# Casting loads on GpSimd's queue, pooling by TensorE, and a second matmul in weight-piece order, in a pooled-attention and feed-forward kernel

## The chip, the cores and the metric

The kernel runs on one core of a Trainium2 chip. The metric is the device time of one execution in microseconds (us), the median of several runs. A core has TensorE (PE, the matmuls; PEld is its loading of weights), VectorE (DVE), ScalarE (ACT), GpSimd (POOL) and SyncE (SP, which here only issues DMAs). A DMA is issued from the queue of one of these engines and carried out by 16 DMA engines that all queues share.

## The reference, cut to what matters

```python
# q, k, v: (8, 8, 576, 64) float32;  w_in: (512, 2048), w_out: (2048, 512) float32
k_p = k.reshape(B, H, Sp, 8, D).mean(axis=3)        # Sp = 72
v_p = v.reshape(B, H, Sp, 8, D).mean(axis=3)
scores = np.matmul(q, k_p.transpose(0, 1, 3, 2)) / np.sqrt(D)
attn = softmax(scores)                               # over the 72 pooled keys
x = np.matmul(attn, v_p)    # then heads side by side: (4608, 512)
h = x @ w_in                # (4608, 2048)
g = h * np.cos(h)
out = g @ w_out             # (4608, 512)
```

## The kernel before

Attention goes batch by batch (8 batches of 576 tokens), the two large matmuls go by tiles of 512 tokens (9 tiles, index t). Batch 0 is attended alone; then tile t runs `up` (first matmul, cosine, product: 8 groups `fp` of two 128-wide chunks, 64 matmuls) and the second matmul, "down" (64 matmuls `down_mm`, by token quarter `ms`, then by chunk `fc`), and between the matmuls of down stand the attention steps of batch t+1, by a hand-written list `fill` of positions (L281, L282). The order on each engine is the program's order; the framework adds the waits.

**Loads.** All loads are issued by SP, float32, into staging tiles: `kv_st` (three buffers, L49), `q_main` and `q_rem` (one each, L50), `w_st` (two, L48), in the order k0, q0, v0, four pieces of w_in, four of w_out, k1, q1, v1, k2 and so on. A weight piece is cast to bfloat16 by DVE (w_in, L259) or POOL (w_out, L264); with two buffers, the third piece is loaded only when the first is cast. q is cast by POOL (`cast_q`, L119, L121). k and v are pooled (8 rows summed) by three additions (L111 to L113): on DVE for batch 0, on POOL for the others.

**Attention of a batch.** `k_transpose` (L161) and `q_transpose` (L140: 16 transposes of 128x128, two heads each) and `q_transpose_rem` (L151) bring k and q to the layout that the matmuls want. Then eight steps: `scores` (L171) and an exponential on ACT (L174, `ex`); `values`, which multiplies `ex` by ones (L183: the sums) and by pooled v (L185), takes ACT's logarithm (L187, `lnc`) and exponential (L189, `inv`) of the sums, and multiplies on DVE (L191) into `xT`, the first matmul's input. `values` uses the one pair of PSUM banks, bank 2, so the next step's sums wait for this step's DVE product.

**Second matmul.** Down of a tile uses two PSUM banks in turn (`obanks`); a token quarter passes over all 16 chunks of `w_out_sb` before the next, so the first quarter already needs the whole of w_out.

Of the kernel before, what the change touches and what calls it, by code (L numbers as in the profile page):

```python
# [19 lines left out]
def kernel(  # L20
# [20 lines left out]
    NSTEP = 2 * KCH  # L41
    assert d_model == 512 and S == 576 and n_tokens % TILE == 0
# [12 lines left out]
    identity = consts.tile([128, 128], BF16, name="identity")  # L55
    make_identity(nc, identity)
    ones = consts.tile([128, D], BF16, name="ones")
    nc.gpsimd.memset(ones, float(POOL))
    half_pi = consts.tile([128, 1], FP32, name="half_pi")
    nc.gpsimd.memset(half_pi, math.pi / 2.0)  # L60

    w_in_sb = wpool.tile([128, KCH, d_ff], BF16, name="w_in_sb")
    w_out_sb = wpool.tile([128, FFCH, d_model], BF16, name="w_out_sb")
# [41 lines left out]
    def pool_kv(b, which, eng, halves=1):  # L105
        st = staged.pop((which, b))
        dst = asb.tile([Sp, H, D], BF16, name=f"{which}p", tag=f"{which}p")
        hs = H // halves
        for i in range(halves):
            s = st[:, i * hs:(i + 1) * hs]  # L110
            eng.tensor_tensor(out=s[:, :, 0:4, :], in0=s[:, :, 0:4, :], in1=s[:, :, 4:8, :], op=ADD)  # L111
            eng.tensor_tensor(out=s[:, :, 0:2, :], in0=s[:, :, 0:2, :], in1=s[:, :, 2:4, :], op=ADD)  # L112
            eng.tensor_tensor(out=dst[:, i * hs:(i + 1) * hs, :], in0=s[:, :, 0, :], in1=s[:, :, 1, :], op=ADD)  # L113
# [221 lines left out]
```

## Time and profile before

| | |
|---|---|
| median of 3 runs | 388.56 us (388.04 to 391.95) |
| profiled execution, own time | 387.81 us |
| its span, first to last instruction | 385.9 us |
| PE busy | 326.0 us (84%) |
| ACT, DVE, POOL busy | 191.9, 167.9, 141.3 us |
| DMA, mean over the span | 120 GB/s, 46.41 MB |
| chain that ended last | PE 75%, DMA 12%, DVE 4%, ACT 3%, POOL 3% |

The profile is one execution. The views used are the busy time by stage (windows of time), the chain of work that ended last in order of time, the timeline of instructions, and the DMA traffic of a stretch. Tile names are the program's, and L140 is line 140 of the kernel above.

### The profile page before, as it was taken

To read this page: it belongs to the slowest core of one execution; us is meant where nothing else is said; L and a number is where in the kernel's file an instruction comes from. 1 tells how busy PE (TensorE), PEld (TensorE's weight loads), DVE (VectorE), ACT (ScalarE), POOL (GpSimd) and SP (SyncE) were. 2 spreads that over 40 slices of the span, in tenths; PEclk is the share of its full clock that TensorE was granted. 3 is DMA by queue.
4 is the path that set the end of the run, shared out by engine and by line. 5 is a ranking of instruction groups with operands and counts; after the bars stand their busy time and mean duration, and the time that the engine had idled before them with its cause. 6 is when DMAs were issued, how large, how long until landed. Compare 5 with 4: busy or idle time off the path is not lost.

```text
span 385.9 us, 4455 instructions
## 1 busy us (share of the span) xinstructions
PE 326.0 (84%) x1728; PEld 134.5 (35%) x1728; DVE 167.9 (44%) x212; ACT 191.9 (50%) x280; POOL 141.3 (37%) x70
## 2 busy tenths in 40 slices
PE   0343775087999999999999999999999999999995
PEld 0211222042345234433443343245334433444442
DVE  2452365021357335622753374347335733642741
ACT  1056415014655766575657565656575576621620
POOL 0200033799927930990198049605850000000000
PEclk9999969568999999999999999999999999999999
DMA  7940689898368319821971395149420010002002
GB/s 187 238 159 0 219 288 282 189 191 196 107 157 191 93 38 204 183 63 59 219 175 27 104 217 132 54 124 197 102 56 27 2 54 27 29 27 75 8 27 82
DMA packets 31469, 46.41 MB, mean 120 GB/s; under 512 B 5337, under 2 KB 13529, under 8 KB 31449
## 3 DMA queue, kind: packets, MB, share of 16 engines
q1 hardware_dynamic: 31448, 46.14, 46.8%
q8 instruction: 13, 0.21, 0.3%
q14 instruction: 8, 0.06, 0.1%
HBM read 36.70 MB, written 9.44 MB: 120 GB/s over the span
## 4 chain that ended last, share of the span: by engine, by line
PE 75%; DMA 12%; DVE 4%; ACT 3%; POOL 3%; SPq 1%; issue 1%; POOLq 0%
PE obank L226 34%; PE bank L218 29%; DMA kv_st<-in_v_dram 5%; PE bank L183 4%; PE bank L171 3%; DMA q_main<-in_q_dram 3%; PE bank L185 2%; DMA w_st<-in_moe_w_in_dram 2%; PE bank L140 2%; DVE xT L191 2%; ACT inv L189 2%; ACT lnc L187 2%; DMA w_st<-in_moe_w_out_dram 1%; POOL kv_st L111 1%; DVE w_in_sb L259 1%
## 5 line engine op out<-in xcount | busy, mean ns | idle before, releaser
L226 PE MATMUL obank<-w_out_sb,g_sb 128*128 128x512 bf16 x576 | 151.5, 387 | 0.0
L218 PE MATMUL bank<-xT,w_in_sb 128*128 128x512 bf16 x576 | 130.6, 389 | 6.7 <-DVE g_sb L223 4.1
L222 ACT ACTIVATE cos<-bank,half_pi 128x1024 f32<-128x1024 f32 x72 | 80.3, 1115 | 78.4 <-PE bank L218 78.4
L223 DVE TENSOR_TENSOR g_sb<-bank,cos 128x1024 bf16<-128x1024 f32 x72 | 88.0, 1224 | 51.4 <-ACT cos L222 51.4
L111 POOL TENSOR_TENSOR kv_st<-kv_st 72x2048 f32<-72x2048 f32 x14 | 63.2, 4518 | 87.4 <-DMA kv_st<-in_k_dram 82.7
L218 PEld LDWEIGHTS <-w_in_sb 128*128 128x128 bf16 x576 | 57.4, 100 | 78.6 <-issue 10.6
L191 DVE TENSOR_TENSOR xT<-bank,inv 128x288 bf16<-128x288 f32 x64 | 29.3, 458 | 94.9 <-ACT inv L189 94.9
L174 ACT ACTIVATE ex<-bank 72x576 bf16<-72x576 f32 x64 | 40.8, 640 | 54.4 <-PE bank L171 53.4
L226 PEld LDWEIGHTS <-g_sb 128*128 128x128 bf16 x576 | 46.3, 98 | 58.3 <-issue 14.4
L187 ACT ACTIVATE lnc<-bank 128x288 f32<-128x288 f32 x64 | 26.3, 411 | 41.5 <-PE bank L185 41.5
L231 DVE COPY o_sb<-obank 128x512 f32<-128x512 f32 x36 | 24.8, 688 | 31.0 <-PE obank L226 31.0
L183 PE MATMUL bank<-ex,ones 72*64 72x288 bf16 x128 | 21.3, 324 | 15.7 <-DVE xT L191 15.2
L112 POOL TENSOR_TENSOR kv_st<-kv_st 72x1024 f32<-72x1024 f32 x14 | 32.9, 2349 | 1.1
L189 ACT ACTIVATE inv<-lnc 128x288 f32<-128x288 f32 x64 | 28.3, 442 | 2.0
L161 PE MATMUL bank<-identity,kp 72*128 72x72 bf16 x32 | 2.8, 208 | 26.0 <-POOL kp L113 14.7
L183 PEld LDWEIGHTS <-ones 72*64 72x64 bf16 x128 | 9.1, 109 | 41.4 <-issue 41.4
L185 PE MATMUL bank<-ex,vp 72*64 72x288 bf16 x128 | 20.6, 309 | 3.2 <-POOL vp L113 2.3
L264 POOL CAST w_out_sb<-w_st 128x2048 bf16<-128x2048 f32 x4 | 7.6, 1894 | 41.8 <-DMA w_st<-in_moe_w_out_dram 41.8
L171 PE MATMUL bank<-qT,kpT 64*72 64x288 bf16 x128 | 21.1, 329 | 1.0 <-DVE qT L143 1.0
L119 POOL CAST q_bf<-q_main 128x2048 bf16<-128x2048 f32 x8 | 15.1, 1889 | 11.8 <-DMA q_main<-in_q_dram 11.8
L171 PEld LDWEIGHTS <-kpT 64*72 64x72 bf16 x128 | 7.4, 110 | 27.7 <-issue 27.7
L143 DVE COPY qT<-bank 128x2048 bf16<-128x2048 bf16 x8 | 9.8, 1225 | 8.9 <-PE bank L140 8.9
(26 smaller groups left out, 96.4 us busy)
## 6 DMA issues: line engine op xcount, KB each, us to landing
q_main<-in_q_dram SPq DMA_DIRECT2D x8, 1024.0 KB
out_dram<-o_sb SPq DMA_DIRECT2D x32, 256.0 KB
kv_st<-in_k_dram SPq DMA_DIRECT2D x7, 1152.0 KB
kv_st<-in_v_dram SPq DMA_DIRECT2D x7, 1152.0 KB
w_st<-in_moe_w_in_dram SPq DMA_DIRECT2D x4, 1024.0 KB
w_st<-in_moe_w_out_dram SPq DMA_DIRECT2D x4, 1024.0 KB
kv_st<-in_k_dram SPq DMA_DIRECT2D x2, 576.0 KB
kv_st<-in_v_dram SPq DMA_DIRECT2D x2, 576.0 KB
```

The lines of the kernel that those rows point to most:

```text
L111: eng.tensor_tensor(out=s[:, :, 0:4, :], in0=s[:, :, 0:4, :], in1=s[:, :, 4:8, :], op=ADD)
L112: eng.tensor_tensor(out=s[:, :, 0:2, :], in0=s[:, :, 0:2, :], in1=s[:, :, 2:4, :], op=ADD)
L171: nc.tensor.matmul(pair[:Sp, hp, :SEG], lhsT=kpT[hp * 64:hp * 64 + 64, pj, :], rhs=qT[hp * 64:hp * 64 + 64, pj, sg * SEG:(sg + 1) * SEG])
L174: nc.scalar.activation(out=ex, in_=pair[:Sp, :, :SEG], func=ACTF.Exp, scale=scale / POOL)
L183: nc.tensor.matmul(cs[hp * 64:hp * 64 + 64, :], lhsT=ones[:Sp, :], rhs=ex[:, hp, :])
L187: nc.scalar.activation(out=lnc, in_=cs, func=ACTF.Ln)
L189: nc.scalar.activation(out=inv, in_=lnc, func=ACTF.Exp, scale=-1.0)
L191: nc.vector.tensor_mul(out=xT[:, pj, c0:c0 + SEG], in0=ao, in1=inv)
L218: nc.tensor.matmul(h[:, j, :], lhsT=w_in_sb[:, ki, fc * 128:(fc + 1) * 128], rhs=xT[:, ki, t * TILE:(t + 1) * TILE], start=(ki == 0), stop ...
L222: nc.scalar.activation(out=cos, in_=h, func=ACTF.Sin, bias=half_pi[:, :1])
L223: nc.vector.tensor_mul(out=g_sb[:, 2 * fp:2 * fp + 2, :], in0=h, in1=cos)
L226: nc.tensor.matmul(obanks[ms % 2], lhsT=g_sb[:, fc, ms * 128:(ms + 1) * 128], rhs=w_out_sb[:, fc, :], start=(fc == 0), stop=(fc == FFCH - 1))
```

## The change

- The weights, q of all batches, and k and v of batches 0 and 1 are loaded by DMAs issued from POOL's queue into bfloat16 tiles; the cast happens in the DMA. Casts on DVE and POOL and the staging of weights go. Each weight piece has a tile of its own (`w_in_sb[0..3]`, `w_out_sb[0..3]`), q has two buffers, the bfloat16 k/v four.
- k and v of batches 2 to 7 still come float32 from SP and are pooled by POOL. All k/v loads are split into partitions 0 to 63 and 64 to 71. The loads of k2 and v2 are now SP's first instructions, without a wait.
- k and v of batches 0 and 1 are pooled by TensorE: `pool_k_mm` (64 matmuls against the identity, 8 of them accumulating into one result, which comes out transposed) and `pool_v_mm` (8 matmuls of 512 columns).
- `q_transpose` now takes one head at a time: 32 transposes of 128x64 a batch in place of 16 of 128x128.
- Batch 0's attention uses all PSUM banks: scores run two steps ahead, the sums alternate between two banks, and the products with v follow four steps later.
- In tile 0, down goes by weight piece (`cg`), then token quarter, into four PSUM banks at once; batch 1's transposes and the pooling of v stand ahead of it, the pooling of k inside `up` behind fp 5.

```diff
-    wst = ctx.enter_context(tc.tile_pool(name="wst", bufs=2))
-    kvst = ctx.enter_context(tc.tile_pool(name="kvst", bufs=3))
-    qst = ctx.enter_context(tc.tile_pool(name="qst", bufs=1))
+    kvb = ctx.enter_context(tc.tile_pool(name="kvb", bufs=4))
+    kvst = ctx.enter_context(tc.tile_pool(name="kvst", bufs=2))
+    qst = ctx.enter_context(tc.tile_pool(name="qst", bufs=2))
     asb = ctx.enter_context(tc.tile_pool(name="asb", bufs=2))
     msb = ctx.enter_context(tc.tile_pool(name="msb", bufs=3))
...
+    def load_kv_cast(b, which, src, halves=1):
+        st = kvb.tile([Sp, H, POOL, D], BF16, name=f"{which}_b", tag="kv_b")
         hs = H // halves
...
+        for j in range(halves):
+            for o, i in by_rows(st[:, j * hs:(j + 1) * hs].rearrange("p h t d -> p h (t d)"),
+                                kv_view(src, b)[j * hs:(j + 1) * hs]):
+                nc.gpsimd.dma_start(out=o, in_=i.rearrange("h p n -> p h n"))
...
     def load_w_in(cg):
-        st = wst.tile([128, KCH, 512], FP32, name="w_st", tag="w_st")
-        nc.sync.dma_start(
-            out=st, in_=moe_w_in[:, cg * 512:(cg + 1) * 512].rearrange("(k p) f -> p k f", p=128))
-        return st
+        nc.gpsimd.dma_start(
+            out=w_in_sb[cg],
+            in_=moe_w_in[:, cg * 512:(cg + 1) * 512].rearrange("(k p) f -> p k f", p=128))
...
+    def pool_k_mm(b, bank, pjs):
+
+        kb = staged["k", b]
+        if ("kpT", b) not in att:
+            att["kpT", b] = asb.tile([128, KCH, Sp], BF16, name="kpT", tag="kpT")
+        ps = bank[:, 0:KCH * Sp].rearrange("p (j n) -> p j n", j=KCH)
+        for pj in pjs:
+            for t in range(POOL):
+                for hp in range(2):
+                    nc.tensor.matmul(ps[hp * 64:hp * 64 + 64, pj, :], lhsT=kb[:, 2 * pj + hp, t, :],
+                                     rhs=identity[:Sp, :Sp], start=(t == 0), stop=(t == POOL - 1))
+        sl = slice(pjs[0], pjs[-1] + 1)
+        nc.vector.tensor_copy(out=att["kpT", b][:, sl, :], in_=ps[:, sl, :])
+
+    def pool_v_mm(b, bank):
+        vb = staged["v", b]
+        for t in range(POOL):
+            nc.tensor.matmul(bank[:Sp, :], lhsT=identity[:Sp, :Sp], rhs=vb[:, :, t, :],
+                             start=(t == 0), stop=(t == POOL - 1))
+        dst = asb.tile([Sp, H, D], BF16, name="vp", tag="vp")
+        nc.vector.tensor_copy(out=dst, in_=bank[:Sp, :].rearrange("p (h d) -> p h d", h=H))
+        pooled["v", b] = dst
...
-        for t in range(4):
-            for pj in range(KCH):
-                nc.tensor.matmul(ps[:, t, pj, :], qb[:, t, 2 * pj:2 * pj + 2, :].rearrange("p h d -> p (h d)"),
-                                 identity, is_transpose=True)
+        for i, pj in enumerate(pjs):
+            for t in range(4):
+                for hp in range(2):
+                    nc.tensor.matmul(ps[hp * 64:hp * 64 + 64, i, t, :], qb[:, 2 * pj + hp, t, :],
+                                     identity, is_transpose=True)
...
+    load_kv_cast(0, "k", k, 2)
...
+    load_q(0, 2)
+    load_kv_cast(0, "v", v)
+    for cg in range(4):
+        load_w_in(cg)
+    load_kv_cast(1, "k", k)
+    load_q(1)
+    load_kv_cast(1, "v", v)
+    for cg in range(4):
+        load_w_out(cg)
+    load_kv(2, "k", k)
+    load_kv(2, "v", v)
...
+    LAG = 4
...
+    for i in range(NSTEP + LAG):
+        if i < NSTEP:
+            sums(0, i, obanks[i % 2])
+            inverse(0, i, obanks[i % 2])
+            if i + 2 < NSTEP:
+                scores(0, i + 2, banks[i % 2])
+        if i == LAG - 1:
+            pool_v_mm(0, banks[2][:, 0, :])
+        if i >= LAG:
+            values(0, i - LAG, banks[2][:, 0, :])
+            normal(0, i - LAG, banks[2][:, 0, :])
...
+            if t == 0 and fp == 5:
+                pool_k_mm(1, obanks[0], range(KCH))
...
+        if t == 0:
+            outs = [obanks[0], obanks[1], banks[2][:, 0, :], banks[2][:, 1, :]]
+            mms = [(ms, fc) for cg in range(4) for ms in range(4) for fc in range(4 * cg, 4 * cg + 4)]
             exp_tables()
+            q_transpose(1, banks[0])
+            q_transpose_rem(1, banks[1][:, 0, :])
+            pool_v_mm(1, banks[1][:, 1, :])
+            main = att_main(1, [banks[0]], banks[1])
+            fill = [(i * 7 // 2, f) for i, f in enumerate(main)]
```

The first place is the head of the load queues. Before, SP's queue begins so (each row one DMA; "x4" four alike):

```order
L77 DMA kv_st<-in_k_dram 72x4x512 x2
L84 DMA q_main<-in_q_dram 128x8x256
L87 DMA q_rem<-in_q_dram 64x8x64
L77 DMA kv_st<-in_v_dram 72x4x512 x2
L92 DMA w_st<-in_moe_w_in_dram 128x4x512 x4
L98 DMA w_st<-in_moe_w_out_dram 128x4x512 x4
L77 DMA kv_st<-in_k_dram 72x8x512
L84 DMA q_main<-in_q_dram 128x8x256
L87 DMA q_rem<-in_q_dram 64x8x64
L77 DMA kv_st<-in_v_dram 72x8x512
```

Now the same loads stand in POOL's queue (`k_b`, `v_b` are the bfloat16 tiles), of which these are some rows, with the waits that the framework gives them; `DMASW0` to `DMASW7` are eight semaphores that POOL's DMAs take in turn:

```order
L87 DMA k_b<-in_k_dram 64x4x512
...
L96 DMA q_main<-in_q_dram 128x4x256
...
L98 DMA q_rem<-in_q_dram 64x4x64
L87 DMA v_b<-in_v_dram 64x8x512 [waits DMASW0_49]
L87 DMA v_b<-in_v_dram 8x8x512 [waits DMASW1_49]
L102 DMA w_in_sb_81<-in_moe_w_in_dram 128x4x512 [waits DMASW2_49]
...
L107 DMA w_out_sb_88<-in_moe_w_out_dram 128x4x512 [waits DMASW7_49]
L96 DMA q_main<-in_q_dram 128x8x256 [waits DMASW0_49,PE_49]
L98 DMA q_rem<-in_q_dram 64x8x64 [waits DMASW1_49,PE_49]
L117 TENSOR_TENSOR kv_st<-kv_st 72x8x256 [waits DMAHW1_49,DMAHW0_49]
```

No load waits for a cast any more; a load waits for the eighth one ahead of it, and POOL's pooling of batch 2 (last row) stands behind all the weight loads.

The second place is TensorE at the beginning of tile 0's down. Before, four matmuls stand ahead of batch 1's k (`kp`, pooled by POOL), and the quarter stays on one output bank:

```order
L218 MATMUL bank_95<-xT,w_in_sb 128x512
L226 LDWEIGHTS g_sb
L226 MATMUL obank_97<-w_out_sb,g_sb 128x512
...
L161 LDWEIGHTS kp
L161 MATMUL bank_96<-identity,kp 128x72
...
L226 LDWEIGHTS g_sb
L226 MATMUL obank_97<-w_out_sb,g_sb 128x512
```

Now the transposes of q and the pooling of v come first, and four matmuls into one bank are followed by four into the next, all with weight piece 0 (`w_out_sb_85`):

```order
L168 MATMUL bank_91<-identity,q_main 64x128
...
L150 MATMUL bank_92<-v_b,identity 72x512
...
L199 MATMUL bank_91<-qT,kpT 72x288
...
L266 MATMUL obank_94<-w_out_sb_85,g_sb 128x512
...
L266 MATMUL obank_95<-w_out_sb_85,g_sb 128x512
```

Nothing of down waits for POOL's additions in tile 0 any more, and the first 16 matmuls need a quarter of w_out.

## Rows read from the trace of the kernel before

**Rows 1.** The page's first line.

```profile
span 385.9 us, 4455 instructions
```

**Rows 2.** Stages in windows: from:to, length, busy us (instructions) by engine, clock, DMA share.

```profile
core 0: us, PE busy (x) PEld busy (x) DVE busy (x) ACT busy (x) POOL busy (x), PEclk, DMA share, GB/s
0.00:18.37 18.37, 2.81 (x25) 2.21 (x25) 6.24 (x9) 1.28 (x1) 3.27 (x10) 1.00 0.91 211
18.37:39.78 21.41, 8.73 (x48) 3.65 (x48) 9.39 (x17) 12.51 (x25) 0.00 (x0) 1.00 0.25 82
39.78:62.59 22.81, 18.66 (x65) 7.46 (x66) 10.98 (x10) 7.80 (x7) 5.68 (x3) 0.85 0.84 288
62.59:107.14 44.55, 26.65 (x138) 9.68 (x137) 9.44 (x16) 15.18 (x27) 37.82 (x17) 0.77 0.76 171
143.71:180.28 36.57, 35.64 (x201) 14.45 (x200) 17.67 (x23) 22.87 (x34) 18.66 (x8) 1.00 0.53 126
```

**Rows 3.** The chain that ended last, in order of time: start us, us, what.

```profile
1.62 11.54 DMA q_main<-in_q_dram
...
40.89 7.70 DMA w_st<-in_moe_w_in_dram
...
61.01 20.08 DMA kv_st<-in_v_dram
81.22 4.51 POOL kv_st L111
...
107.14 13.81 PE bank L218 x64
```

**Rows 4.** Timeline of one attention step of batch 0: start us, us, instruction [idle before].

```profile
24.28 0.41 ACT L187 ACTIVATE lnc<-bank 128x288 f32<-128x288 f32 x1 [1.50 <-PE bank L185]
...
24.73 0.44 ACT L189 ACTIVATE inv<-lnc 128x288 f32<-128x288 f32 x1
...
25.07 0.63 ACT L174 ACTIVATE ex<-bank 72x576 bf16<-72x576 f32 x1
25.20 0.46 DVE L191 TENSOR_TENSOR xT<-bank,inv 128x288 bf16<-128x288 f32 x1 [1.70 <-ACT inv L189]
```

**Rows 5.** Timeline of tile 0's up on TensorE.

```profile
39.78 7.09 PE L218 MATMUL bank<-xT,w_in_sb 128*128 128x512 bf16 x24 [2.60 <-DVE w_in_sb L259]
```

**Rows 6.** DMA traffic of 41 to 50, of 60 to 82 and of 43 to 47 us.

```profile
DMA packets 1210, 2.41 MB, mean 268 GB/s; under 512 B 32, under 2 KB 32, under 8 KB 1210
...
DMA packets 3309, 4.63 MB, mean 211 GB/s; under 512 B 584, under 2 KB 1636, under 8 KB 3309
...
DMA packets 742, 1.46 MB, mean 366 GB/s; under 512 B 27, under 2 KB 27, under 8 KB 742
```

**Rows 7.** Timeline of TensorE in tile 2's down: transposes and a step of attention.

```profile
158.22 0.29 PE L161 MATMUL bank<-identity,kp 72*128 72x72 bf16 x4
158.35 1.03 PE L226 MATMUL obank<-w_out_sb,g_sb 128*128 128x512 bf16 x4
159.22 1.06 PE L140 MATMUL bank<-identity,q_bf 128*128 128x128 bf16 x16
160.11 1.03 PE L226 MATMUL obank<-w_out_sb,g_sb 128*128 128x512 bf16 x4
...
164.04 0.31 PE L183 MATMUL bank<-ex,ones 72*64 72x288 bf16 x2
164.18 0.29 PE L185 MATMUL bank<-ex,vp 72*64 72x288 bf16 x2
164.41 0.60 PE L226 MATMUL obank<-w_out_sb,g_sb 128*128 128x512 bf16 x2
```

**Rows 8.** Timeline of DVE: the last two products of tile 2's up.

```profile
156.98 1.22 DVE L223 TENSOR_TENSOR g_sb<-bank,cos 128x1024 bf16<-128x1024 f32 x1 [0.50 <-ACT cos L222]
158.71 1.23 DVE L223 TENSOR_TENSOR g_sb<-bank,cos 128x1024 bf16<-128x1024 f32 x1 [0.50 <-ACT cos L222]
```

**Rows 9.** Timeline of SP's queue: the issue of one load of 512 short rows.

```profile
109.37 2.24 SPq L87 DMA_DIRECT2D q_rem<-in_q_dram  x1
```

More of the change, by code (lines that the diff above doesn't have):

```diff
@@ L53 @@
     psum = ctx.enter_context(tc.tile_pool(name="psum", bufs=1, space=bass.MemoryType.PSUM))
[L55 to L63, printed above, removed]
+    w_in_sb = [wpool.tile([128, KCH, 512], BF16, name=f"w_in_sb{i}") for i in range(4)]
+    w_out_sb = [wpool.tile([128, 4, d_model], BF16, name=f"w_out_sb{i}") for i in range(4)]
     xT = wpool.tile([128, KCH, n_tokens], BF16, name="xT")
@@ L100, in load_w_out, with pool_kv @@
-        return st
+        nc.gpsimd.dma_start(
+            out=w_out_sb[cg],
+            in_=moe_w_out[cg * 512:(cg + 1) * 512, :].rearrange("(f p) m -> p f m", p=128))
     pooled = {}
-    def pool_kv(b, which, eng, halves=1):
-        st = staged.pop((which, b))
+    def pool_kv(b, which, eng):
+        s = staged.pop((which, b))
         dst = asb.tile([Sp, H, D], BF16, name=f"{which}p", tag=f"{which}p")
[L108 to L113, printed above, removed]
-        pooled[which, b] = dst
@@ L164, in k_transpose, with scores @@
         att["kpT", b] = kpT
-    def scores(b, i):
+    def scores(b, i, pair):
         pj, sg = i // 2, i % 2
         kpT, qT = att["kpT", b], att["qT", b]
-        pair = banks[(i + 1) % 2]
         for hp in range(2):
@@ L193, in att_steps, with sums, inverse @@
-    def att_steps(b):
-        early = [lambda: k_transpose(b, banks[2][:, 0, :]),
-                 lambda: q_transpose(b, banks[0]),
-                 lambda: q_transpose_rem(b, banks[2][:, 1, :])]
-        main = [lambda: scores(b, 0)]
+    def sums(b, i, cs):
+        ex = att["ex", b, i]
+        for hp in range(2):
+            nc.tensor.matmul(cs[hp * 64:hp * 64 + 64, :SEG], lhsT=ones[:Sp, :], rhs=ex[:, hp, :])
+    def inverse(b, i, cs):
+        lnc = asb.tile([128, SEG], FP32, name="lnc", tag="lnc")
+        nc.scalar.activation(out=lnc, in_=cs[:, :SEG], func=ACTF.Ln)
+        inv = asb.tile([128, SEG], FP32, name="inv", tag="inv", bufs=EX)
+        nc.scalar.activation(out=inv, in_=lnc, func=ACTF.Exp, scale=-1.0)
+        att["inv", b, i] = inv
@@ new lines, in values, with normal, step @@
+    def values(b, i, ao):
+        ex = att.pop(("ex", b, i))
+        vp = pooled["v", b]
+        pj = i // 2
+        for hp in range(2):
+            nc.tensor.matmul(ao[hp * 64:hp * 64 + 64, :SEG], lhsT=vp[:, 2 * pj + hp, :], rhs=ex[:, hp, :])
+    def normal(b, i, ao):
+        pj, sg = i // 2, i % 2
+        c0 = b * S + sg * SEG
+        nc.vector.tensor_mul(out=xT[:, pj, c0:c0 + SEG], in0=ao[:, :SEG], in1=att.pop(("inv", b, i)))
+    def step(b, i, pair):
+        cs, ao = pair[:, 0, :], pair[:, 1, :]
+        sums(b, i, cs)
+        values(b, i, ao)
+        inverse(b, i, cs)
+        normal(b, i, ao)
```

182 lines of the change are left out of this document (87 added, 95 removed).

## The prediction

> **What bounds the kernel now.** The windows by stage come first. From 107.14 us to the end of the span, 385.9 us [rows 1, 3], TensorE is the bound: a whole tile, up and down with attention, takes 36.57 us, of which PE is busy 35.64 [rows 2]. Ahead of that lie 107.14 us for work that at the later pace would be one tile plus batch 0's attention: PE is busy 2.8, 8.7, 18.7 and 26.7 us in the four stages of the head [rows 2]. The chain in order of time says what those stages wait for: q0's load, until 13.16 us; then attention; then the third piece of w_in, which found no free staging buffer before 40.89 us; at last k1, q1 and v1, which stand behind all weights in SP's queue, v1 landing at 81.1, and POOL's additions behind it [rows 3]. In batch 0's attention (18.37 to 39.78) every engine is mostly idle, as are the DMA engines, at a share of 0.25 [rows 2]: of a step, ACT needs 0.45 + 0.34 + 0.63 = 1.42 us (starts of the three functions, and the last one's length), but the next logarithm waits 1.5 us because the sums wait for DVE's product in the one bank pair [rows 4]. So the head holds the gain; the stretch behind 107.14 can only be lengthened, by work added to PE.
>
> **The loads.** Up to the last piece of w_out the new head moves: k0, q0, v0, k1, q1, v1 at 1.18 MB each (8 x 576 x 64 x 4 bytes), eight weight pieces at 1.05, and SP's k2 and v2, 2.36 MB, which are issued at once; 17.83 MB as read. I count the bytes that are read, as for a plain load; no row shows a casting DMA. The rate's bounds are the nearest rows: 211 GB/s, where k, v and q dominate, and 366, where weight pieces move alone [rows 6]. The mix of 8.39 MB at 366 and 9.44 at 211 gives 264; the stretch with w_in and w_out mixed shows 268 [rows 6], and I take 268. A load that ends at byte N of the queue is usable at 3.5 + N/268: q0 before was ready at 13.16 [rows 3], with 2.23 MB ahead at 211 GB/s [rows 2], so 2.6 us of start, and I add 0.9 because POOL has to write the descriptors. SP's 2.36 MB I put wholly ahead of q0's end. Ready then: q0 (4.72 MB) 21.1; v0 25.5; w_in 29.4, 33.3, 37.2, 41.2; k1 45.6; q1 50.0; v1 54.4; w_out 58.3, 62.2, 66.1, 70.0 us. No load waits for a buffer, only for the eighth ahead of it, which leaves several megabytes in flight; I cost that at nothing, since traffic under way covers it.
>
> **TensorE and ACT in the head.** q0's second half needs 16 half-width transposes, the rest of q and two scores, 1.8 us at the slow clock of this stage: 22.9. Eight steps at ACT's 1.42, a last product of 0.46 [rows 4] and 0.7 us for the pooling of v, which stands between two sums on PE: up starts at 35.5 (before: 39.78 [rows 5]). Up takes 13.81 at full pace [rows 3]. Before, its first 24 matmuls took 7.09 us [rows 5] where 24/64 of 13.81 is 5.18: 1.9 us, eight matmuls at 1.2 instead of 2.4 GHz, which I keep. Pooling k1 by 64 small matmuls: four transposes of 72 columns took 0.13 us from start to start [rows 7], so 2.1; by the whole 0.29 that those rows show, 4.7; I take 3.2, nearer the start-to-start value. It starts at 47.8, k1 being there. Up ends at 54.4.
>
> Ahead of down now: the bank of the last group but one is free 0.7 us after up's end, that of the last 2.4 after (tile 2's up ended at 143.71 + 13.81 = 157.52; its products ended at 158.20 and 159.94 [rows 2, 3, 8]). The transposes of q fit between; then 0.3 for the rest of q and eight matmuls of 512 columns for v, 1.7: down starts 4.4 after up, at 58.8, with w_out's first piece there at 58.3. Its 64 matmuls take 13.81; a whole tile's 36.57 less 27.62 leaves 8.95 for attention, of which 1.3 are transposes [rows 7] and 0.9 a last wait; eight steps, about 7.0. A quarter takes 5.2, later than each piece of w_out lands (64.0 against 62.2, 74.4 against 70.0). Up of tile 1 starts at 79.6 instead of 107.14: **27.5 us less**. Where DVE's and POOL's casts go, nothing stays; POOL's additions for batch 2 now stand behind the weight loads, but are wanted only at tile 1's down, near 93 us, and take 16 us a batch.
>
> **What is added behind it.** Each of the batches 2 to 7 transposes q by 32 matmuls of half width in place of 16; on PE nothing covers it. The 16 took 0.89 us (159.22 to 160.11). Two half-width matmuls over different columns overlap: the pair on the sums took 0.14 us, where one of 288 columns at 2.4 GHz is 0.12 [rows 7]. So the 32 take between 0.89 and twice that, and 0.2 for the change of shape on both sides (the pair on v took 0.23, 0.1 of it before the full-width matmul [rows 7]). Bounds 0 and 1.1 us a batch; I take 0.6, the middle: **3.6 us more**. The Trainium skill (TensorE: Matmul & The Clock Gate, Weight-path perf modes and LDWEIGHTS) speaks against this edit: weights of 128 columns get a fast load, others load at columns/1.2 ns, an estimated 1.7 us for 32 loads of 64, so some 1.0 a batch and 6 in all. The pair's rows do not decide it, since 288 columns cover its loads.
>
> Sum against the profiled execution's own 387.81: 387.81 - 27.5 + 3.6 = 363.9. The median stands 0.75 above that execution: 364.7, and I say **365**. At 366 GB/s q0 is ready at 16.4, everything behind it is ready earlier and PE sets the pace: up of tile 1 at 74.9, and with transposes at nothing 356.3. At 211 the last piece of w_out lands at 88.0, up of tile 1 starts at 93.2: 378.2.
>
> **The rivals.** *Casting loads run slow: slower than before.* The whole stream now leaves POOL's one queue, written row by row, 9,472 rows up to the end of w_out. Up of tile 1 may start 3.6 us ahead of 107.14 for the gain to be eaten; a last quarter of 5.2 and 3.5 of start leave 94.8 us, so it decides below 188 GB/s or above 10 ns a row. For it: stages of before ran at 171 and 211 GB/s [rows 2] with SP's queue. Against it: SP's issue of 512 short rows took 2.24 us, 4.4 ns a row [rows 9], 41 us for all. At 150 GB/s the last piece lands at 122.4, up starts at 127.6: 387.81 + 20.5 + 3.6 + 0.75 = 412. The Trainium skill (SBUF — State Buffer, Who interferes with whom) has one mechanism for it, POOL's descriptor writing blocked while DVE copies within SBUF in its two-port modes; the DVE casts that do so are removed here and the copies left read PSUM, so by that rule it would not happen, which no run here shows.
>
> *The load rate is near 200: little change.* Between 188 and 211 the loads set the pace and the time is 378 to 392, say 383. For it: 64 partitions by 8 heads of k and v are still half of the bytes, and they moved at 211 or less.
>
> *SP's k2 and v2 do not hold q0 up.* If POOL's loads are served first, all of them are 8.8 us earlier: 356. Against it: SP issues within the first microsecond and POOL must write first.
>
> **How the numbers follow.** Forecast (211 to 366 GB/s) 0.62, its own range 356 to 378. Little change 0.14, half of it still over 1% faster. Slow loads 0.18. k2/v2 behind 0.06. So faster by over 1% (under 384.7, about what this measurement tells from no change) 0.75, within 1% 0.07, slower 0.18. The range from 355 to 389 leaves out the slow loads and a bit of either end.
>
> **What would show it.** Right: first scores near 23 us; ACT without gaps of over 0.5 us in batch 0's attention; up of tile 0 near 35 and of tile 1 near 80; tiles 1 to 6 at about 37.2 us; DMA at 250 GB/s or more until 70 us. Wrong: PE waiting for w_out pieces in tile 0's down, or POOL's queue solid with DMA issues beside DMA engines that idle (slow loads); tiles at 36.6 or at 38 (transposes); stalls of PE in tile 0 that let its clock fall.

## The result, and the profile after

| | before | after |
|---|---|---|
| median of the runs compared | 389.02 us (388.04 to 391.95) | 374.17 us (373.32 to 375.26) |
| ratio, 95% interval | | 0.961 (0.955 to 0.967) |
| span of the profiled execution | 385.9 us | 371.6 us |
| up of tile 1 starts | 107.14 us | 91.49 us |
| from there to the end of the span | 278.8 us | 280.1 us |

Four runs of each are compared, one more of the kernel before than in the table ahead. The kernel became 3.9% faster, 14.9 us; 365 was predicted, in a range from 355 to 389. The head gave 15.65 us where 27.5 were forecast, and what follows lost 1.3 where 3.6 were forecast.

The windows of after answer [rows 2]. A window ends where a stage ends: first scores, start and end of tile 0's up, start of its attention and down, start of tile 1's up; the last row is a stretch of one later tile's length. Columns as in [rows 2]; the DMA share is the sum of the packets' times over that of 16 engines, so it passes 1 where packets overlap.

```profile
core 0: us, PE busy (x) PEld busy (x) DVE busy (x) ACT busy (x) POOL busy (x), PEclk, DMA share, GB/s
0.00:25.98 25.98, 4.62 (x98) 3.88 (x99) 1.44 (x4) 1.28 (x1) 11.12 (x24) 1.00 1.24 161
25.98:43.88 17.90, 13.36 (x61) 5.05 (x60) 4.71 (x10) 11.90 (x25) 5.72 (x9) 1.00 1.43 182
43.88:60.66 16.78, 16.76 (x128) 7.62 (x129) 8.73 (x9) 7.80 (x7) 13.89 (x7) 1.00 1.43 182
60.66:67.94 7.28, 4.86 (x45) 2.50 (x45) 3.22 (x4) 2.40 (x2) 6.13 (x5) 0.74 0.35 38
67.94:91.49 23.55, 22.01 (x114) 7.44 (x114) 6.14 (x12) 13.29 (x25) 0.00 (x0) 0.94 0.26 48
128.20:164.90 36.70, 35.77 (x217) 14.30 (x216) 17.73 (x23) 22.88 (x34) 17.77 (x8) 1.00 0.56 110
```

The long stretches with an idle TensorE of [rows 2] (18.66 busy of 22.81, 26.65 of 44.55) are gone: up and down of tile 0 now run nearly dense. But the first scores come at 25.98 us, 7.6 later than before (18.37), and TensorE is busy for 4.62 us of that time. Batch 0's attention takes 17.90 us, and the stretch between up and down 7.28 with a granted clock of 0.74.

| step | predicted | measured |
|---|---|---|
| first scores | 22.9 | 25.98 |
| batch 0's attention, to the start of up | 12.6 | 17.90 |
| up of tile 0 | 18.9 | 16.78 |
| from up to down | 4.4 | 7.28 |
| down of tile 0 | 20.8 | 23.55 |
| up of tile 1 starts | 79.6 | 91.49 |

The chain in order of time (start us, us, what), against [rows 3]:

```profile
5.79 19.14 DMA q_main<-in_q_dram
...
31.60 3.56 PE bank L150 x8
...
43.88 12.05 PE bank L258 x48
...
64.44 3.57 PE bank L150 x8
...
91.49 13.60 PE bank L258 x63
...
128.29 13.81 PE bank L258 x64
...
165.09 13.81 PE bank L258 x64
```

The weights' staging and the loads of k1 and v1, which [rows 3] show in it, no longer stand in the chain. In their place stand q0's load, 19.14 us from its issue, and twice the pooling of v by eight matmuls (L150). The last two rows are the starts of two later tiles' up: a tile takes 36.80 us, 36.57 before [rows 2].

### The profile page after: what moved, and what is told of

It reads as the page before. It is cut to its first block, busy times and chain, and to the rows that moved or that the text cites. A ratio compares the mean times of both kernels' runs of the same rounds, so it can differ in the third digit from the quotient of the medians.

```text
span 371.6 us, 4965 instructions
## 1 busy us (share of the span) xinstructions
PE 332.1 (89%) x1992; PEld 137.7 (37%) x1992; DVE 156.4 (42%) x201; ACT 191.8 (52%) x280; POOL 124.2 (33%) x80
## 4 chain that ended last, share of the span: by engine, by line
PE 86%; DMA 5%; DVE 3%; ACT 3%; POOL 1%; issue 1%; DVEq 0%; POOLq 0%
PE bank L258 34%; PE obank L266 34%; DMA q_main<-in_q_dram 5%; PE bank L199 4%; PE bank L208 4%; PE bank L222 3%; PE bank L168 2%; PE bank L150 2%; PE bank L266 2%; DVE xT L227 2%; ACT inv L214 1%; ACT lnc L212 1%; POOL k_b L87 1%; DVE o_sb L271 1%; DVE qT L171 0%
## 5 line engine op out<-in xcount | busy, mean ns | idle before, releaser
L266 PE MATMUL obank<-w_out_sb,g_sb 128*128 128x512 bf16 x544 | 141.4, 383 | 0.0
L258 PE MATMUL bank<-xT,w_in_sb 128*128 128x512 bf16 x576 | 127.6, 382 | 0.0
L117 POOL TENSOR_TENSOR kv_st<-kv_st 72x2048 f32<-72x2048 f32 x12 | 54.2, 4519 | 110.5 <-DMA kv_st<-in_k_dram 110.5
L202 ACT ACTIVATE ex<-bank 72x576 bf16<-72x576 f32 x64 | 41.0, 641 | 49.9 <-PE bank L199 48.5
L212 ACT ACTIVATE lnc<-bank 128x288 f32<-128x288 f32 x56 | 23.0, 411 | 32.2 <-PE bank L222 32.2
L271 DVE COPY o_sb<-obank 128x512 f32<-128x512 f32 x34 | 23.4, 687 | 29.4 <-PE obank L266 29.4
L118 POOL TENSOR_TENSOR kv_st<-kv_st 72x1024 f32<-72x1024 f32 x12 | 28.2, 2349 | 0.9
L208 PE MATMUL bank<-ex,ones 72*64 72x288 bf16 x112 | 17.5, 307 | 6.3 <-DVE xT L227 6.3
L222 PE MATMUL bank<-ex,vp 72*64 72x288 bf16 x128 | 20.1, 303 | 3.1 <-DVE xT L227 3.1
L199 PE MATMUL bank<-qT,kpT 64*72 64x288 bf16 x128 | 21.5, 331 | 0.4 <-DVE qT L183 0.4
L142 PE MATMUL obank<-identity,k_b 72*64 72x72 bf16 x128 | 3.6, 227 | 19.2 <-DMA k_b<-in_k_dram 19.2
L168 PE MATMUL bank<-identity,q_main 128*64 128x128 bf16 x256 | 9.7, 232 | 2.9 <-DMA q_main<-in_q_dram 2.1
L171 DVE COPY qT<-bank 128x2048 bf16<-128x2048 bf16 (+1 forms) x9 | 9.9, 1105 | 5.1 <-PE bank L168 5.1
## 6 DMA issues: line engine op xcount, KB each, us to landing
w_in_sb<-in_moe_w_in_dram POOLq DMA_DIRECT2D x4, 512.0 KB, 13.2
w_out_sb<-in_moe_w_out_dram POOLq DMA_DIRECT2D x4, 512.0 KB, 15.5
```

Source lines behind the costliest of these rows:

```text
L199: nc.tensor.matmul(pair[:Sp, hp, :SEG], lhsT=kpT[hp * 64:hp * 64 + 64, pj, :], rhs=qT[hp * 64:hp * 64 + 64, pj, sg * SEG:(sg + 1) * SEG])
L202: nc.scalar.activation(out=ex, in_=pair[:Sp, :, :SEG], func=ACTF.Exp, scale=scale / POOL)
L208: nc.tensor.matmul(cs[hp * 64:hp * 64 + 64, :SEG], lhsT=ones[:Sp, :], rhs=ex[:, hp, :])
L222: nc.tensor.matmul(ao[hp * 64:hp * 64 + 64, :SEG], lhsT=vp[:, 2 * pj + hp, :], rhs=ex[:, hp, :])
L258: nc.tensor.matmul(h[:, j, :], lhsT=w_in_sb[fc // 4][:, ki, (fc % 4) * 128:(fc % 4 + 1) * 128], rhs=xT[:, ki, t * TILE:(t + 1) * TILE], st ...
L266: nc.tensor.matmul(o, lhsT=g_sb[:, fc, ms * 128:(ms + 1) * 128], rhs=w_out_sb[fc // 4][:, fc % 4, :], start=(fc == 0), stop=(fc == FFCH - 1))
```

## Where the head lost: readings of the trace of after

Batch 0's attention on ScalarE (start us, us, instruction, idle before; compare [rows 4]):

```profile
26.56 0.65 ACT L202 ACTIVATE ex<-bank 72x576 bf16<-72x576 f32 x1 [24.54 <-PE bank L199]
...
29.31 0.40 ACT L212 ACTIVATE lnc<-obank 128x288 f32<-128x288 f32 x1
...
30.62 0.40 ACT L212 ACTIVATE lnc<-obank 128x288 f32<-128x288 f32 x1
...
35.58 0.41 ACT L212 ACTIVATE lnc<-obank 128x288 f32<-128x288 f32 x1 [2.25 <-PE obank L208]
...
39.48 0.44 ACT L214 ACTIVATE inv<-lnc 128x288 f32<-128x288 f32 x1
```

A step takes 1.31 us (29.31 to 30.62) without a gap, as the prediction had it with 1.42. Then ACT idles once for 2.25 us, waiting for sums that stand on TensorE behind the pooling of v. TensorE around that, and at the end of the stage:

```profile
31.53 3.62 PE L150 MATMUL bank<-v_b,identity 72*72 72x512 bf16 x8
...
42.36 0.45 PE L222 MATMUL bank<-ex,vp 72*64 72x288 bf16 x2 [0.62 <-DVE xT L227]
43.43 0.45 PE L222 MATMUL bank<-ex,vp 72*64 72x288 bf16 x2 [0.62 <-DVE xT L227]
```

Eight matmuls of 512 columns in 3.6 us are 0.45 us each, which is the lower level of 1.2 GHz; in a dense stretch the same eight take 1.89 (see the experiments). TensorE was busy for 4.62 of the 25.98 us ahead of this stage. The granted clock of the first two rows above reads 1.00 all the same, so here the level is told from the lengths of the matmuls, not from that column. And each product with v waits for DVE to empty the one bank that they all use, 1.07 us a step, so that they end 4 us behind ACT, whose last `inv` is done at 39.92.

TensorE between up and down:

```profile
61.38 1.08 PE L168 MATMUL bank<-identity,q_main 128*64 128x128 bf16 x32 [0.74 <-DVE g_sb L263]
63.11 0.27 PE L180 MATMUL bank<-identity,q_rem 64*128 64x64 bf16 x4 [0.64 <-DVE g_sb L263]
64.44 3.57 PE L150 MATMUL bank<-v_b,identity 72*72 72x512 bf16 x8 [1.06 <-DVE qT L183]
67.94 0.45 PE L199 MATMUL bank<-qT,kpT 64*72 64x288 bf16 x2
```

Three waits, 2.44 us together, and then again eight matmuls of 0.45 us. The third wait is for the copy of the rest of q, whose bank is in one pair with that of the pooling of v. Last, the waits of TensorE in tile 0's down (67.94 to 91.49), of which none is for a load:

```profile
engine line waited for: us in total, times, longest us
PE bank L266 <- DVE o_sb L271: 0.8, 1, 0.8
PE bank L208 <- DVE xT L227: 0.7, 1, 0.7
```

## The experiments

Each experiment is one execution, the last one six. Executions of one kernel lie up to 3.9 us apart (388.04 to 391.95 before), so the readings go by stages.

### What holds up q0

```diff
-    load_kv(2, "k", k)
-    load_kv(2, "v", v)
+    load_kv(2, "k", k, nc.gpsimd)
+    load_kv(2, "v", v, nc.gpsimd)
```

> Of the changed kernel only the place of k2 and v2 differs: they leave SP's queue, where they were the first instructions, and are issued by POOL behind the last piece of w_out. Theory (the 2.36 MB of k2 and v2 stand ahead of q0 in the DMA engines): the second half of q0 is there at 16 +-2 us in place of 24.98, the first scores start near 17 instead of 25.99, all that follows keeps its length, so up of tile 0 starts near 35 instead of 43.88 and the span is about 363 instead of 371.6. Rival (the casting queue itself is slow at its start, its rows being short and written one by one): q0 stays within 2 us of 25 and the span within 2 us of 371.6.

Measured: q0's last half lets TensorE start at 12.18 us in place of 24.98, span 358.5. Both gains are larger than the theory's: 12.8 us for 2.36 MB. The chain of this kernel:

```profile
5.79 6.34 DMA q_main<-in_q_dram
...
31.42 11.41 PE bank L258 x47
...
78.24 9.06 PE bank L258 x42
```

The same load takes 6.34 us instead of 19.14, and all that follows moves with it. How the two queues share is seen in the DMA traffic between 6 and 10 us (queue: packets, MB, and its packets' time as a share of 16 engines'). After:

```profile
DMA packets 464, 0.70 MB, mean 175 GB/s; under 512 B 31, under 2 KB 214, under 8 KB 464
...
q1 hardware_dynamic: 273, 0.51, 79.7%
q0 software_dynamic: 191, 0.19, 40.0%
```

With k2 and v2 late:

```profile
DMA packets 1412, 0.67 MB, mean 168 GB/s; under 512 B 352, under 2 KB 1412, under 8 KB 1412
...
q0 software_dynamic: 1412, 0.67, 138.1%
```

POOL's queue (q0, software) moves 191 packets in 4 us beside SP's (q1, hardware), 1412 alone. Its bytes are counted as written: half of q is 131,072 numbers, and the profile lists 256 KB for it, two bytes each. So alone it moves what would be 1.34 MB as read, and beside SP's queue 0.38, with SP's 0.51 that is 0.89 for both. How the two share changes as it goes on: each moves 287 packets from 10 to 14 us, and from 14 to 18 POOL's moves 622, SP's 241; no run says by what rule. With k2 alone at the head of SP's queue:

```diff
     load_kv(2, "k", k)
-    load_kv(2, "v", v)
+    load_kv(2, "v", v, nc.gpsimd)
```

> As the changed kernel, but only k2 stays at the head of SP's queue (1.18 MB); v2 goes behind the last piece of w_out on POOL's queue. With both there the last of q0 let TensorE start at 24.98 us, with neither at 12.18. Theory (SP's bytes take time of the same 16 DMA engines, in proportion): 18.6 +-1.5 us, span about 365. Rival (any transfer of SP's queue at the head holds up the casting queue for a fixed time, or the two queues share well and only the last of SP's bytes hurts): nearer than 2 us to one of the two ends.

Measured: 17.02 us, span 363.4. Neither end, so the delay grows with SP's bytes; a little below the theory's 17.1 to 20.1: the first 1.18 MB cost 4.8 us, the second 8.0. Why the second costs more isn't settled.

### Batch 0's attention

The products with v on two banks, the sums on one:

```diff
-            sums(0, i, obanks[i % 2])
-            inverse(0, i, obanks[i % 2])
+            sums(0, i, obanks[0])
+            inverse(0, i, obanks[0])
...
-            values(0, i - LAG, banks[2][:, 0, :])
-            normal(0, i - LAG, banks[2][:, 0, :])
+            vb = obanks[1] if i % 2 else banks[2][:, 0, :]
+            values(0, i - LAG, vb)
+            normal(0, i - LAG, vb)
```

> Of the changed kernel only batch 0's PSUM banks differ: all sums on one bank, the products with v in turn on two. Theory (the products wait for DVE on one bank, 1.07 us a step, and end 4 us behind ACT): up of tile 0 starts at 40.6 +-0.5 us in place of 43.88, and the span is 3.3 us shorter, 368.3. Rival (ACT and the pooling of v set the pace, and sums on one bank hold up the logarithms): ACT's steps grow from 1.31 us and up starts at 43 or later.

Measured: up of tile 0 starts at 41.73, span 369.7; the stage takes 16.20 us (25.53 to 41.73) in place of 17.90, a gain of 1.7 where 3.3 were expected. ACT keeps its 1.31 us a step, so the rival is out. The last four products now follow each other by some 0.55 us instead of 1.07; the stall of ACT ahead of them, behind the pooling of v, is untouched (2.56 us here), and the products before can't run ahead of it.

The old arrangement, back in the changed kernel:

```diff
...
+    main = att_main(0, [banks[0], banks[1]], banks[2])
+    for n, f in enumerate(main):
+        if n == 2:
+            pool_v_mm(0, obanks[0])
+        f()
```

> Of the changed kernel only batch 0's attention is put back to the form before: each step's sums and product with v in one bank pair, the next step behind them; the pooling of v stands behind the first two scores. Theory (the new arrangement is worth what a step of before, 2.155 us, loses against ACT's 1.31): q0 being there at 25, the pooling of v ends near 31.6, eight steps take 17.2, and up of tile 0 starts at 49 in place of 43.88, the span is 377. Rival (the one bank for the products with v has taken the gain back): up starts at 45.5 or earlier.

Measured: up's first matmul starts at 48.80 (43.81 in the same view of after), span 376.0. The theory holds: the new arrangement is worth about 5 us (4.4 in the span), even with the pooling of v in ACT's way and the products on one bank. Of the 5, 1.57 are a wait of TensorE for v0, which the old form needs in its first step.

### Between up and down

```diff
+            if t == 0 and fp == 6:
+                pool_v_mm(1, obanks[1])
...
-            pool_v_mm(1, banks[1][:, 1, :])
```

> Of the changed kernel only the pooling of v1 moves: from ahead of tile 0's down, where its eight matmuls took 3.57 us at half clock behind a wait of 1.06, into up of tile 0 behind group 6, on a bank that is free there. Theory (the stretch ahead of down is long because PE has little to do there and then works at half clock): the stretch from up's end to down's first matmul falls from 7.3 to 3 +-0.7 us, up grows by 1.8, and down's first nine matmuls run at full clock, 2 less; span about 367. Rival (the bank waits on the last products set the stretch and the clock falls anyway): stretch 5 or more, down still 23.5, span 370 or more.

The stages of this kernel: up, between, down.

```profile
44.24:63.13 18.89, 18.83 (x136) 8.62 (x138) 9.77 (x10) 7.80 (x7) 16.37 (x8) 1.00 1.25 168
63.13:66.90 3.77, 1.29 (x36) 1.14 (x37) 2.55 (x3) 2.40 (x2) 3.33 (x4) 1.00 0.02 2
66.90:89.21 22.31, 20.48 (x110) 7.29 (x113) 5.46 (x11) 13.29 (x25) 0.00 (x0) 1.00 0.30 52
```

Between up and down 3.77 us remain (7.28 before the edit; 3 +-0.7 was expected), up is 2.1 longer, down 1.2 shorter at a clock of 1.00. In the span that is 2.3 us, half of what the theory forecast: the wait for the last product of up stays (1.45 us on DVE), so does that of 1.06 for the copy of the rest of q, now ahead of the first scores, and down takes 22.3, not 21.5. The eight matmuls took 1.89 us in up against 3.57 ahead of down:

```profile
59.51 1.89 PE L150 MATMUL obank<-v_b,identity 72*72 72x512 bf16 x8
```

The granted clock is 1.00 in all three stages, where it was 0.74 and 0.94 in the last two.

### The order of tile 0's down

```diff
-            mms = [(ms, fc) for cg in range(4) for ms in range(4) for fc in range(4 * cg, 4 * cg + 4)]
+            mms = [(ms, fc) for ms in range(4) for fc in range(FFCH)]
```

> Of the changed kernel only the order of tile 0's down differs: by token quarter and then by chunk, as before the change, on the same four banks. Theory (all of w_out has landed by 63 us, before down starts at 67.94, so the order by weight piece buys nothing): no wait of PE for w_out, down within 1 us of 23.55, shorter rather than longer since the copies of the outputs are spread. Rival (the order by weight piece is what lets down start early): PE waits for the last pieces in the first quarter and down takes 3 us or more longer.

Measured: first scores to up of tile 1 take 24.4 us against 23.55, at a granted clock of 0.90 against 0.94; span 372.3. It is not shorter, as the theory would have had it; the wait for a copy is still there. The waits of TensorE in it:

```profile
PE bank L266 <- DVE o_sb L271: 0.8, 1, 0.8
PE bank L208 <- DVE xT L227: 0.7, 1, 0.7
PE obank L266 <- issue: 0.4, 2, 0.2
```

None is for w_out. From the start of tile 0's up to that of tile 1's this kernel takes 48.5 us; in runs with the weight-piece order that stretch took 46.8 (k2 and v2 late) to 48.5 (full-width transposes). So in the changed kernel as it is, the weight-piece order gains nothing that stands out from what runs differ by: w_out has landed. It wasn't tried where the head is fast enough to meet w_out.

### The transposes of q

```diff
-                for hp in range(2):
-                    nc.tensor.matmul(ps[hp * 64:hp * 64 + 64, i, t, :], qb[:, 2 * pj + hp, t, :],
-                                     identity, is_transpose=True)
+                nc.tensor.matmul(ps[:, i, t, :],
+                                 qb[:, 2 * pj + t % 2, 2 * (t // 2):2 * (t // 2) + 2, :].rearrange("p t d -> p (t d)"),
+                                 identity, is_transpose=True)
```

> Of the changed kernel only the transposes of q differ: 16 a batch at full width, each over two neighbouring rows of one head, in place of 32 at half width; half of the transposed q lands on the wrong partitions, so that the attention computed is not the reference's, while the work on every engine is the same in kind and size. Theory (the starts in the trace: 32 take 1.02 us where 16 took 0.89): the six tiles become 0.13 us shorter each, span about 370.6. Rival one (the prediction's 0.6 us a batch): span 368. Rival two (the 1.0 us a batch estimated from the Trainium skill, TensorE: Matmul & The Clock Gate, Weight-path perf modes and LDWEIGHTS): span 365.6.

Measured: from the start of tile 1's up to the end 278.75 us (92.45 to 371.2), against 280.1 with half-width transposes and 278.8 in the kernel before. So the transposes are the whole of what the tiles lost, 1.35 us, 0.22 a batch: more than the 0.13 between the starts, less than half of 0.6, a quarter of 1.0. (The head of this run was 0.96 longer, which hides most of it in the span.) The rows of after:

```profile
143.89 1.08 PE L168 MATMUL bank<-identity,q_main 128*64 128x128 bf16 x32
144.91 1.04 PE L266 MATMUL obank<-w_out_sb,g_sb 128*128 128x512 bf16 x4
```

and with 16 at full width:

```profile
144.53 1.06 PE L167 MATMUL bank<-identity,q_main 128*128 128x128 bf16 x16
145.43 1.03 PE L266 MATMUL obank<-w_out_sb,g_sb 128*128 128x512 bf16 x4
```

32 half-width ones follow each other by 32 ns (1.02 us for all). The Trainium skill (TensorE: Matmul & The Clock Gate, Weight-path perf modes and LDWEIGHTS) has weights of 64 columns load without the fast path; for 32 such loads one after the other it would give an estimated 1.7 us. The trace does not show that cost: 1.02 us here.

### Is the cast in the DMA needed?

The kernel before, with other loads and buffers only:

```diff
-    wst = ctx.enter_context(tc.tile_pool(name="wst", bufs=2))
-    kvst = ctx.enter_context(tc.tile_pool(name="kvst", bufs=3))
+    wst = ctx.enter_context(tc.tile_pool(name="wst", bufs=4))
+    kvst = ctx.enter_context(tc.tile_pool(name="kvst", bufs=2))
...
-    w_stage = [load_w_in(0), load_w_in(1)]
+    w_stage = [load_w_in(cg) for cg in range(4)]
+    load_kv(1, "k", k)
+    load_q(1)
+    load_kv(1, "v", v)
...
-        if cg + 2 < 4:
-            w_stage.append(load_w_in(cg + 2))
+    pool_kv(1, "k", nc.gpsimd)
+    cast_q(1, nc.gpsimd)
     for cg in range(4):
         st = load_w_out(cg)
...
-    load_kv(1, "k", k)
-    load_q(1)
-    load_kv(1, "v", v)
-    pool_kv(1, "k", nc.gpsimd)
-    cast_q(1, nc.gpsimd)
```

> The kernel before, with its plain float32 loads from SP, its casts on DVE and POOL and its additions for k and v, but with k1, q1 and v1 loaded and k1 and q1 treated ahead of w_out, four staging buffers for weights in place of two, and two for k and v in place of three. Theory (the head's gain comes from the order of the loads and from staging, not from the cast in the DMA nor from pooling on TensorE): up of tile 0 keeps its start at 39.8 and takes 14 to 16 us, POOL is done with v1 near 71, and up of tile 1 starts at 84 +-4 in place of 107.14; span 363 +-4, no longer than the changed kernel's 371.6. Rival (POOL's additions and casts, 26 us in a row behind the landing of k1, hold up tile 0's down): up of tile 1 at 95 or later, span 374 or more.

Measured: span 370.2, up of tile 1 at 91.44. Neither theory's number: 15.7 us faster than the kernel before, as fast as the changed kernel, but 7 short of the forecast. What it lost is a hole in up: TensorE waits 3.0 us for a cast of w_in and then 6.55 at DVE, whose four casts now take 13.98 us in a row. The casts, all of one size (count and duration ns: least, median, most):

```profile
L262 DVE CAST w_in_sb<-w_st x4: 1217/3741/5526, 38.5 to 48.4; 128x2048 bf16<-128x2048 f32 x4
```

and POOL at that time, adding up k1:

```profile
39.06 5.03 POOL L111 TENSOR_TENSOR kv_st<-kv_st 72x2048 f32<-72x2048 f32 x1 [23.39 <-DMA kv_st<-in_k_dram]
44.17 3.21 POOL L112 TENSOR_TENSOR kv_st<-kv_st 72x1024 f32<-72x1024 f32 x1
```

To tell whether the two are in each other's way, k1 and q1 were put behind the casts of w_out on POOL:

```diff
-    pool_kv(1, "k", nc.gpsimd)
-    cast_q(1, nc.gpsimd)
     for cg in range(4):
         st = load_w_out(cg)
         nc.gpsimd.tensor_copy(out=w_out_sb[:, cg * 4:(cg + 1) * 4, :], in_=st)
+    pool_kv(1, "k", nc.gpsimd)
+    cast_q(1, nc.gpsimd)
```

> The reordered form of the kernel before, where four casts of w_in on DVE took 13.98 us while POOL added up k1 at the same time (one such cast took 1.23 in the kernel before, beside an idle POOL); now k1 and q1 are treated by POOL only behind the casts of w_out. Theory (DVE's casts and POOL's additions, both within SBUF, slow each other down): the four casts take 5 us, up of tile 0 runs from 40 to 55 without a hole, POOL's first addition takes 4.5 in place of 5.03 and its second 2.34 in place of 3.21; what follows waits for k1, pooled near 66. Rival (the casts are slow because the loads of w_out write to SBUF at the same time, or wait for data): the casts stay above 10 us in all.

DVE, with the same columns:

```profile
L262 DVE CAST w_in_sb<-w_st x4: 1217/1220/1221, 38.6 to 42.0; 128x2048 bf16<-128x2048 f32 x4
```

and POOL:

```profile
64.06 4.49 POOL L111 TENSOR_TENSOR kv_st<-kv_st 72x2048 f32<-72x2048 f32 x1
68.63 2.34 POOL L112 TENSOR_TENSOR kv_st<-kv_st 72x1024 f32<-72x1024 f32 x1
```

Each cast is back at 1.22 us, the additions at 4.49 and 2.34, and up runs without a hole from 39.91 (15.39 us). The loads go on during the casts (DMA share 0.91 from 38.5 to 43.3 us), so the rival is out. The theory holds: DVE's casts took up to 4.5 times as long beside POOL's additions. (In all this order is slower, span 379.3, since down then waits 15.2 us for k1.) The Trainium skill (SBUF — State Buffer, Who interferes with whom) has DVE's copies within SBUF in the two-port modes and GpSimd exclude each other for whole instructions; the durations agree with it: the longest cast, 5.53, is its own 1.22 and 4.3 more, about the length of POOL's first addition. Casting in the DMA takes these casts off both engines, so this collision can't occur. What it is worth as a faster load no run separates: with k2 and v2 late, TensorE starts on the last of q0 at 12.18 us, while before it started on q0 at 15.16, behind POOL's cast.

### Together

Three of the edits above in one kernel (k2 and v2 late, two banks for the products, the pooling of v1 in up):

> Of the changed kernel three edits together, each measured alone before: k2 and v2 behind w_out (span 371.6 to 358.5), two banks for batch 0's products with v (to 369.7), the pooling of v1 inside up (to 369.3). Theory (the three holes lie one behind the other on TensorE's path and have nothing to do with each other): gains of 13.1, 1.9 and 2.3 add up, span 354.3 +-0.7. Rival (once q0 is early the head meets the loads of k1, v1 or w_out, so that the later gains are lost): span 356.5 or more, with PE waiting for a load in up or down of tile 0.

Measured: span 355.1, up of tile 1 at 74.6, no wait for a load in up or down. (Between the two a wait of 1.4 us is put down to k2's load, but the transposes behind it don't read k2, and the wait for the last product of up, 1.45 long with the pooling of v1 in up alone, ends there too.) So nothing new took the place of the holes. The sum misses by 0.8, the size of what differs from run to run in the single gains: q0's last half came at 24.52 with two banks and at 24.98 without, and from the start of tile 0's up to that of tile 1's it is 46.8 us with k2 and v2 late alone, 47.6 in the changed kernel.

And all that the runs point to, with the main lines:

```diff
+    late = {5: (0, 1), 6: (2, 3), 7: (4, 5, 6), 8: (7,)}
...
-        if i == LAG - 1:
-            pool_v_mm(0, banks[2][:, 0, :])
+        if 1 <= i <= 4:
+            pool_v_mm(0, banks[2][:, 0, :], range(2 * i - 2, 2 * i))
+        for n in late.get(i, ()):
+            vb = obanks[1] if n % 2 else banks[2][:, 0, :]
+            values(0, n, vb)
+            normal(0, n, vb)
...
+            if t == 0 and fp == 6:
+                pool_v_mm(1, obanks[1])
+                q_transpose_rem(1, obanks[0])
...
-            fill = [(i * 7 // 2, f) for i, f in enumerate(main)]
+            fill = [(8 + 3 * i, f) for i, f in enumerate(main)]
```

> Everything that the runs so far point to: k2 and v2 behind w_out; the pooling of v0 spread by two matmuls over four steps of ACT in place of eight at once; products with v on two banks and two to three a step; the pooling of v1 and the rest of q1 inside up, the other transposes of q1 on a bank free at up's end; attention in tile 0's down from its ninth matmul on; the third quarter's copy behind the fourth quarter's last matmul. Theory (after q0's arrival ACT paces batch 0 at 1.31 us a step, then TensorE has work without a hole): up of tile 0 starts at 26 (31.42 with k2 and v2 late alone), ends at 41.5, down starts within 1.5 us of that, up of tile 1 starts at 66.7 +-2; span 347, time 349 us. Rival (the loads bound then, at some 206 GB/s as written: w_in's last pieces near 27 and w_out's four between 40 and 49): PE waits for a piece and up of tile 1 starts at 71 or later, time 353 or more.

Measured: 352.57 us (351.49 to 352.82) against 389.23, ratio 0.905 (0.9025 to 0.9077). Its stages: to the first scores, attention, up, down with what stands ahead of it.

```profile
0.00:13.17 13.17, 4.82 (x102) 4.09 (x103) 1.52 (x5) 1.28 (x1) 11.31 (x24) 1.00 0.98 124
13.17:27.57 14.40, 12.83 (x59) 4.20 (x57) 4.15 (x10) 11.82 (x25) 4.70 (x7) 1.00 1.25 205
27.57:46.34 18.77, 18.77 (x142) 8.59 (x144) 10.29 (x12) 8.34 (x8) 5.64 (x8) 1.00 1.27 207
46.34:69.50 23.16, 21.70 (x146) 8.16 (x146) 7.21 (x12) 15.67 (x27) 17.05 (x7) 1.00 0.76 110
```

Tile 1's up starts at 69.5, 2.8 later than the theory's 66.7 and 0.8 outside its bound, and PE waits for no load, so the rival is out too. Up starts 1.6 later than forecast, since on TensorE, at 1.2 GHz by the lengths of its matmuls, two matmuls of the pooling make a step 1.76 us instead of 1.31; up takes 18.8 with the pooling of k1 and v1 in it, where the forecast had 15.5, which 13.81 and some 1.7 for the clock fill without any pooling. This version beats both kernels: 36.7 us less than before, of which the changed kernel had 14.9.

## Why the prediction was off by 9

The direction and the mechanism were right: the head holds the gain, loads set its start, and TensorE sets the rest. The sizes of five steps were not.

- **q0's arrival, predicted 21.1, measured 24.98 (first scores 22.9 and 25.98).** One term was mis-sized. SP's 2.36 MB "wholly ahead of q0's end" were put at 8.8 us and cost 12.8 (k2 and v2 late). The rest of the term was right: 21.1 less 8.8 is 12.3, and with k2 and v2 away q0 is usable at 12.18. Two queues at once moved less of what was wanted first than the bytes say: by the prediction's own count, 4.72 MB by 24.98 us are 220 GB/s, near its lower bound of 211. The rival that k2 and v2 don't hold q0 up falls. (The 22.9 had the first scores behind it; ACT's first exponential starts at 26.56, so counted in the same way 0.6 of what the next stage lost belongs here.)
- **Batch 0's attention, predicted 12.6, measured 17.9.** ACT's pace was right. The 0.7 us for the pooling of v was the failed step: it reckoned eight matmuls as a short stall, while at the stage's 1.2 GHz they take 3.6 us and cost ACT 2.25. Not seen at all: the products with v, which the changed code puts on one bank, need 1.07 us a step when they come in a row, so that the last one ends 4.0 us behind ACT, where 0.46 was allowed. Two banks gave back 1.7; with the pooling spread and the products packed closer as well it was 3.5 (17.9 to 14.4).
- **Up, predicted 18.9, measured 16.78.** The 1.9 for the clock were right (16.78 less 1.16 for the pooling of k is 15.6, against 13.81). The pooling of k1 by 64 small matmuls took 1.16 us, not 3.2: 18 ns each, below the lower bound taken from [rows 7], 2.1.
- **Between up and down, predicted 4.4, measured 7.28.** The pooling of v1 was put at 1.7, at full clock, and took 3.57 at half; the wait of 1.06 for the copy of the rest of q was missed. Moved into up, the pooling took 1.89; the wait stayed.
- **Down, predicted 20.8, measured 23.55.** At full clock it takes 22.3 (pooling of v1 in up), so 1.2 are clock. The other 1.5 are the length of the two waits shown above: 0.8 for the third quarter's copy, in one bank pair with the fourth, and 0.7 ahead of the last sums. The second was known: the prediction read "0.9 a last wait" out of a later tile and left it out of this sum.
- **The transposes, predicted 3.6, measured 1.35.** The middle of 0 and 1.1 was too high; the value lay near the lower bound, where the pairs of half-width matmuls overlap as the pair on the sums does [rows 7].

Of the signs that the prediction named, a tile of 36.80 us lies nearer to its 36.6 (wrong) than to its 37.2 (right), ACT has a gap of 2.25 us, and TensorE's stalls in tile 0 did let its clock fall, to a granted 0.74 between up and down.

In sum the head is 3.1 + 5.3 - 2.1 + 2.9 + 2.7 = 11.9 us later than forecast, and what follows 2.25 shorter: 9.6, against the 9.5 between the sum of 364.7 and the median. Of the rivals, slow casting loads fell: POOL issued each in 0.6 to 0.9 us, and none of the matmuls of tile 0 waited for a weight. A load rate near 200 fell with it: behind q0 the loads are faster than the prediction's 268, up to 205 GB/s as written, 410 as read (30 to 36 us). So the forecast of w_out's last piece, 70 us, was late: the DMA share is already down to 0.35 after 60.66. The eighth-load waits cost nothing that shows: the DMA share is 1.24 to 1.43 in the stages in which POOL waits so.

What the change's parts gave: reordering the loads and adding buffers alone (without the cast in the DMA, pooling on TensorE or the piece order) reached the same 91.4 us for tile 1's up. That the two are equal is chance: in that kernel q0 does not stand behind k2 and v2, and with these out of the way the changed kernel gets there at 78.24, 13.2 us sooner. So the new parts together are worth more than the new order of the loads in the old form; how much is due to the cast in the DMA and how much to pooling on TensorE has no run. Of the new arrangement, batch 0's is worth about 5 us, the piece order nothing that stands out; what k2 and v2 at the head of SP's queue cost, 13 us, took back nearly as much as the whole change brought.

## What to carry to other kernels

Count at time zero not only what is on the path but every transfer that is issued at once: a load that nobody needs for 50 us can cost the first one 13. Eight matmuls in a stretch where TensorE had gaps ran at 1.2 GHz, 3.6 us, and took 1.89 inside a dense stretch, so such work should be priced by where it stands; results that are produced and emptied in a row followed each other by 1.07 us on one bank and by some 0.55 on two. Before a new mechanism is credited with a gain, the old one with its loads in the new order is worth a run.

## What the runs showed of the hardware that was not expected

- A queue of POOL's casting loads alone moved 205 GB/s as written, 410 as read, from 30 to 36 us; plain weight loads had 366 in [rows 6] and 393 from 50 to 54 us of before. From 44 to 50 us, with 358 packets under 512 B in place of 45, it was 156 as written, 312 as read; plain loads of k, v and q had 211 [rows 6]. The stretch from 30 to 36 us:

```profile
DMA packets 1244, 1.23 MB, mean 205 GB/s; under 512 B 45, under 2 KB 1244, under 8 KB 1244
```

- Beside SP's plain loads it moved 0.19 MB as written in 4 us, alone 0.67 (6 to 10 us).
- DVE's casts within SBUF and POOL's additions stretch each other: 1.22 us to as much as 5.53 on DVE, 4.49 to 5.03 and 2.34 to 3.21 on POOL.
- 64 accumulating matmuls of 72 columns by 64-column weights took 1.16 us in up, 18 ns each, weight loads included.
- The stretch behind the head is the same to 0.5 us in all kernels with one kind of transposes: 280.0 to 280.5 with 32 a batch, 278.75 to 278.8 with 16.
